# Spectral products of a gated state-space kernel: four real products or three

## The chip, the cores and the metric

The kernel runs on one core of a Trainium2 chip. The metric is the device time of one execution in microseconds. Before the change the median of three executions is 379.08 us (379.05 to 380.93).

## The reference

Two branches read the same input `x` (2048 positions by 1024 channels) and are mixed by a gate. Branch `a` is a diagonal complex state-space recurrence between two projections. Branch `b`, the one the change touches, is a long convolution by FFT:

```python
kv  = k_shift * v                           # k_shift: four taps over k
y_f = rfft(pad(kv)) * rfft(pad(ssm_k))      # complex products, each channel for itself
y   = irfft(y_f)[:S] + kv * ssm_D
b   = x * y
g   = sigmoid((x * gate_w).sum(-1))
out = g * a + (1 - g) * b
```

## The kernel before

**Engines.** TensorE (PE) does the transforms of the convolution as matmuls with tables of cosines and sines, and the projections of branch `a`. VectorE (DVE) does the products of spectra, then the scans of the recurrence. ScalarE (ACT) moves results out of PSUM. SyncE (SP) issues loads and stores, GpSimd (POOL) issues transfers that add into their target (`gather`). Nearly every instruction goes through a helper (`mm`, `tt`, `act`, `move`, `gather`) which chains it behind the one before on its engine, so the order on each engine is the order of the Python text. All these have line 95 in the profile, and are told apart by the tiles they write and read.

**Chunks.** The convolution runs over 8 chunks of 128 channels. The sequence is cut into 4 blocks of 512, and each block is transformed on its own. So a chunk has a spectrum `KH[c]` of the kernel and `VH[c]` of the product k by v, each with a real and an imaginary part, 4 blocks and 512 frequencies: 2 x 4 x 512 elements in each partition. `products(c)` is a complex product and a convolution over blocks at once: output block b sums K block a times V block b - a. The K spectrum already holds the overlap of neighbouring blocks: for chunks 1 to 6 `fwd_K` adds it on PE, for chunk 7 `overlap_K` adds it on DVE (six operations).

**The loop over c = 0 to 6** (line 1190), in which chunk c is multiplied while chunk n = c + 1 is transformed and chunk nn = c + 2 is prepared. `products` and others are generators; `step` runs one up to its next `yield`. In the order of the text, for c from 1:

- `inverse(c - 1)`: 16 matmuls `psz` on the finished spectrum `whole[c - 1]`, which `products(c - 1)` has written over the V spectrum (`Vh` in the profile). The first eight need its first half.
- `step(tv)`: mirror of chunk n's product, `mirror` on PE and `lo` on ACT.
- four steps of `products(c)`, then the rest of `tv`: `ev` on DVE and a gather `ks<-lo`.
- `fwd_K(n)`: matmuls `psk`; the fifth step of `products(c)`; folds of K for nn; the load of `v` for nn, for c = 2 to 4 held by a write of ACT into the tile (`hold`) until ACT gets there; the taps of nn on PE and their copy `ks<-taps` on ACT; loads of k for the chunk after.
- the sixth step, `run(prod)` (the rest), `overlap_K` where it is due, and only then `times_v(nn)`, whose first operation is `ks<-ks,v`: taps of nn times `v` of nn, 2048 elements.
- `fwd_V(n)`: 16 matmuls `psv`, half on `ev`, half on `ks` after its gather; ACT copies them into `Vh`.

Between these stand matmuls of branch `a` (`even`, `odd`). Chunk 7 is multiplied after the loop. There `by_dma` is false and all sums are made on DVE; for chunks 1 to 6 one sum, of 3072 elements `acc<-wkh`, is made by a gather.

**Tiles.** `sums` (`acc` in the profile) has 8192 elements in each partition, `WK` (`wkh`) 7168; `t` is a spare tile. K lies in `BT[2]` or `BT[3]`.

Of the kernel before, what the change touches and what calls it, by code (L numbers as in the profile page):

```python
# [9 lines left out]
ALU = mybir.AluOpType  # L10
ACT = mybir.ActivationFunctionType
BF16 = mybir.dt.bfloat16
# [8 lines left out]
def kernel(  # L21
# [62 lines left out]
    def u4(shape, dt, name):  # L84
        return s5p["wu"].tile(shape, dt, name=name, tag="u4")
# [12 lines left out]
    def mm(o, l, r, first, last):  # L98
        put("pe", nc.tensor.matmul, o, lhsT=l, rhs=r, start=first, stop=last)

    def bc(ap, shape):
        return ap.to_broadcast(shape)
# [3 lines left out]
    def tt(o, a, b, op):  # L106
        put("dve", V.tensor_tensor, out=o, in0=a, in1=b, op=op)
# [19 lines left out]
    def gather(o, i):  # L127
        put("pool", nc.gpsimd.dma_start, out=o, in_=i, accum_op=ALU.add)
# [355 lines left out]
        act(TC[:, 2 * g:2 * g + 2], y, func=ACT.Sin, bias=pih, scale=-TWO_PI)  # L484

    KH, VH = {}, {}

    eos, kss = {}, {}

# [146 lines left out]
    def fwd_K(c, fis=range(NFI)):  # L636
        eo = eos["k", c]
        if c not in KH:
            KH[c] = spectrum("K", c)
        for fi in fis:  # L640
            fsl = slice(fi * 128, (fi + 1) * 128)
            ps = ps2([128, 2, 4, 128], "psk")
            for cc in range(2):
                tab = CF if cc == 0 else SF
                for mt in range(2):
                    mm(ps[:, cc], tab[:, mt, fsl], eo[:, cc, mt], mt == 0, c == NC - 1 and mt == 1)
                for mt in range(0 if c == NC - 1 else 2):
                    tb2 = (SF, NCF)[cc][:, mt, fsl]
                    mm(ps[:, cc, 1:4], tb2, eo[:, 1 - cc, mt, 0:3], False, mt == 1)
            act(of_tile(KH[c], fi), ps, func=ACT.Copy)  # L650
# [15 lines left out]

    def overlap_K(c):

        K = KH[c][0]
        for b in (3, 2, 1):  # L670
            tt(K[:, 0, b], K[:, 0, b], K[:, 1, b - 1], ALU.add)
            tt(K[:, 1, b], K[:, 1, b], K[:, 0, b - 1], ALU.subtract)

    def fwd_V(c, fis=range(NFI)):
        eo = eos["v", c]
# [8 lines left out]
                    mm(ps[:, cc], tab[:, mt, fsl], eo[cc][:, mt], mt == 0, mt == 1)  # L684
            act(of_tile(VH[c], fi), ps, func=ACT.Copy, scale=2.0 / 1024.0)

    def products(c, h=0, home=u4, by_dma=True):

        K, Vt = (x[c][h].rearrange("p c b f d -> p c b (f d)") for x in (KH, VH))
        w = K.shape[3]  # L690
        A = sums[:, :, h * 2048:h * 2048 + 8 * w].rearrange("p k (c b x) -> p k c b x", c=2, x=w)

        def mult(a, t):

            if len(t.shape) == 2:
                t = t.rearrange("p (k y) -> p k y", k=2)
            t = t.rearrange("p k (c b x) -> p k c b x", c=2, x=w)
            k_ = bc(K[:, :, a:a + 1], [128, 2, 8 - 2 * a, w])
            v_ = bc(Vt[:, :, 0:4 - a].rearrange("p c b x -> p c (b x)")[:, None], [128, 2, 2, (4 - a) * w])
            tt(t, k_, v_, ALU.mult)  # L700
            return t

        n1 = WK[:, h * 3072:h * 3072 + 12 * w].rearrange("p (k c b x) -> p k c b x", k=2, c=2, b=3)

        def first(k):

            for f in range(2 if c == 0 and h == 0 else 1):
                x = slice(f * 128, f * 128 + 128) if c == 0 and h == 0 else slice(0, w)
                tt(A[:, k, :, :, x], bc(K[:, k:k + 1, 0:1, x], [128, 2, 4, x.stop - x.start]), Vt[:, :, :, x], ALU.mult)

        def second(k):
            tt(n1[:, k], bc(K[:, k:k + 1, 1:2], [128, 2, 3, w]), Vt[:, :, 0:3], ALU.mult)

        if by_dma:
            first(0)
            yield
            second(0)
            gather(A[:, 0, :, 1:], n1[:, 0])
            yield
            first(1)  # L720
            yield
            second(1)
            if c > 0:
                yield
            tt(A[:, 1, :, 1:], A[:, 1, :, 1:], n1[:, 1], ALU.add)
        else:
            mult(0, sums)
            yield
            mult(1, WK[:, 0:6144])
            yield  # L730
            tt(A[:, :, :, 1:], A[:, :, :, 1:], n1, ALU.add)
        if c > 0:
            yield
        if c > 0:
            n3 = mult(3, home([128, 4 * w], BF16, "t"))
            n2 = WK[:, 3072:7168].rearrange("p (k c b x) -> p k c b x", k=2, c=2, b=2)
            for k in (1, 0):
                tt(n2[:, k], bc(K[:, k:k + 1, 2:3], [128, 2, 2, w]), Vt[:, :, 0:2], ALU.mult)
            yield
            for k in (1, 0):  # L740
                tt(n2[:, k, :, 1:], n2[:, k, :, 1:], n3[:, k], ALU.add)
            tt(A[:, 1, :, 2:], A[:, 1, :, 2:], n2[:, 1], ALU.add)
            yield
            for i in (0, 1):
                tt(A[:, 0, i, 2:], A[:, 0, i, 2:], n2[:, 0, i], ALU.add)
            yield
        else:
            n2 = mult(2, home([128, 8 * w], BF16, "t"))
            n3 = mult(3, home([128, 4 * w], BF16, "t"))
            yield  # L750
            tt(n2[:, :, :, 1:], n2[:, :, :, 1:], n3, ALU.add)
            tt(A[:, 1, :, 2:], A[:, 1, :, 2:], n2[:, 1], ALU.add)
            yield
            tt(A[:, 0, :, 2:], A[:, 0, :, 2:], n2[:, 0], ALU.add)
            yield
        tt(A[:, 1, 1], A[:, 0, 0], A[:, 1, 1], ALU.subtract)
        tt(A[:, 1, 0], A[:, 0, 1], A[:, 1, 0], ALU.add)
        if c == 0 and h == 0:
            return
        t2 = sums[:, 1]  # L760
        if c > 0:
            lo, hi = (A[:, 1, :, :, i * 256:(i + 1) * 256] for i in range(2))
        else:
            lo, hi = (t2[:, i * 2048:(i + 1) * 2048].rearrange("p (c b x) -> p c b x", c=2, x=256) for i in range(2))
        to = whole[c].rearrange("p (a c b x) -> p a c b x", a=2, c=2, b=4)
        tt(to[:, 0], lo, hi, ALU.subtract)
        tt(to[:, 1], lo, hi, ALU.add)

    def inverse(c):

        G = whole.pop(c).rearrange("p (a c b f d) -> p a c b f d", a=2, c=2, b=4, d=128)
        for par in range(2):
            ps = ps2([128, 2, 4, 128], "psz")
            for j in range(2):
                tl = 2 * par + j
                for fi in range(2):
                    for cc, tab in enumerate((CI, SI)):
                        mm(ps[:, j], tab[:, fi, tl * 128:(tl + 1) * 128], G[:, par, 1 - cc, :, fi],
                           fi == 0 and cc == 0, fi == 1 and cc == 1)
            cv = cv_pool.tile([128, 2, 4, 128], BF16, name="cv")  # L780
            act(cv, ps, func=ACT.Copy)
            move(cv_scr[c, :, 2 * par:2 * par + 2], cv)
            yield
# [337 lines left out]
    def step(gen):  # L1121
        next(gen, None)

    def run(gen):
        for _ in gen:
            pass

    def steps(gen, n):
        for _ in range(n):
            step(gen)  # L1130
# [34 lines left out]
    step(turns)  # L1165
    taps(1, dg1)
    step(columns)
    p0 = products(0, 0)
    steps(p0, 3)
    run(columns)  # L1170
    step(sp)
# [18 lines left out]
    for c in range(NC - 1):  # L1190
        n, nn = c + 1, c + 2
        if c == 0:
            load("kn", 2)
            load("kT", 2)
            load("v", 2)
            load_BT(0, 0)
            load_xT(0, (0,))
            p1 = products(0, 1)
            fwd_K(n, (0, 1))
            steps(p0, 2)  # L1200
            run(tv)
            dg = dgs(nn, True)
            steps(p1, 2)
            step(p0)
            step(p1)
            run(p0)
            taps(nn, dg)
            step(sp)
            fwd_K(n, (2, 3))
            step(p1)  # L1210
            step(sp)
            fwd_V(n)
            run(p1)
            run(fold_K(nn))
            tv = times_v(nn)
            step(tv)
            load("kn", 3)
            load("kT", 3)
            load_BT(0, 1)
            apart = spread(3)  # L1220
            step(apart)
            load_xT(0, (1,))
            run(apart)
            continue
# [66 lines left out]
                run(apart)  # L1291
        step(prod)
        run(fk)
        run(prod)
        if n == NC - 1:
            overlap_K(n)
        if nn < NC:
            tv = times_v(nn)
            step(tv)
            step(parts)  # L1300
        else:
            run(next(tiles))
            CT[0] = ld.tile([128, 2, D], BF16, name="CTa", tag="ld")
            hold(CT[0][:, 0, 0:1])
            load_CT(0)
            load_BT(2, 0)
            load_BT(2, 1)
            run(next(tiles))
            run(next(tiles))
# [55 lines left out]

    s5p["last"] = room

    prod, back = products(c, 0, room, False), inverse(c - 1)
    run(old)
    steps(prod, 3)  # L1370
    run(turns_U[3])
    run(next(tiles))
    steps(turning[0], 2)
# [238 lines left out]
```

## Time and profile before

| what | us |
|---|---|
| median of 3 executions | 379.08 |
| the profiled execution, its own time | 381.19 |
| its span, first to last instruction | 379.4 |
| PE busy | 373.6 |
| DVE busy | 368.0 |
| ACT busy | 303.6 |
| POOL busy | 78.0 |

The profile is of one execution, whose own time is 1.8 us above its span, and 2.1 us above the median. In its timeline each row has a start, a length, the engine, the operation with its tiles (out<-in) and shape, how many were merged, and in brackets the idle time ahead of it with what ended it. Lengths of neighbours on an engine overlap by some 0.08 us on DVE and by more on PE, so what an operation costs is the distance from its start to the next one's. The groups give a sum, a mean length and the idle time before. "SPq" rows are issues of transfers; when a transfer has landed stands in the view of DMA issues.

### The profile page before, as it was taken

The page shows a single profiled execution, that of the slowest core. Times are in us where ns is not written, and L with a number is a line of the kernel's source. Part 1 is how long each engine was busy: PE and PEld are TensorE (multiplying, and loading weights), DVE is VectorE, ACT ScalarE, POOL GpSimd, SP SyncE. Part 2 cuts the span into 40 slices and gives each one's busy share as a digit, 9 for nine tenths or more (in the row PEclk, how much of TensorE's full clock was granted, in tenths as well). Part 3 has the DMA queues.
Part 4 walks back from the last instruction along what each step waited for, and adds up shares of the span by engine and source line. Part 5 has one row for each costly group of instructions (what it writes and reads, how often), then busy time and mean ns, then how long its engine had stood idle before and what let it go on. Part 6 is the DMA issues. An engine that isn't in the chain of part 4 may idle for free.

```text
span 379.4 us, 6680 instructions
## 1 busy us (share of the span) xinstructions
PE 373.6 (98%) x2469; PEld 202.4 (53%) x2469; DVE 368.0 (97%) x596; ACT 303.6 (80%) x465; POOL 78.0 (21%) x106
## 2 busy tenths in 40 slices
PE   8999999999999999999999999999999999999996
PEld 5666457566584756754454444444445444444444
DVE  8899999999999999999999999999999999999984
ACT  5779998998989999777999699977979968936301
POOL 4011020020301102022012014122426322532000
PEclk9999999999999999999999999999999999999999
DMA  7879999999999998999999999946999998997223
GB/s 168 162 117 232 209 210 209 226 214 212 223 191 193 214 192 177 187 208 151 188 209 226 228 199 246 211 70 119 185 248 157 268 248 178 189 244 125 57 83 111
DMA packets 125827, 70.99 MB, mean 187 GB/s; under 512 B 104601, under 2 KB 107553, under 8 KB 125794
## 3 DMA queue, kind: packets, MB, share of 16 engines
q1 hardware_dynamic: 112416, 45.90, 55.4%
q0 software_dynamic: 12256, 24.38, 37.8%
q10 hardware_dynamic: 1122, 0.28, 0.4%
q8 instruction: 19, 0.31, 0.3%
q14 instruction: 14, 0.11, 0.1%
HBM read 15.48 MB, written 8.39 MB: 63 GB/s over the span
## 4 chain that ended last, share of the span: by engine, by line
PE 91%; DMA 6%; ACT 2%; SPq 0%; issue 0%; DVE 0%; ACTq 0%
PE psy L95 29%; PE both L95 22%; PE psk L95 10%; PE taps L95 6%; PE psv L95 6%; PE psz L95 5%; PE even L95 4%; PE odd L95 3%; DMA kT<-in_B_k_dram 3%; PE foldk L95 3%; DMA kT<-kT 2%; DMA kB<-kT 1%; ACT Vh L95 1%; PE p L95 1%; PE mirror L95 1%; ACT hr L95 1%
## 5 line engine op out<-in xcount | busy, mean ns | idle before, releaser
L95 PE MATMUL psy<-CT,U 128*128 128x512 bf16 (+1 forms) x426 | 93.2, 374 | 0.0
L95 PEld LDWEIGHTS <-U 128*128 128x128 bf16 x492 | 48.1, 98 | 55.6 <-issue 0.3
L95 PEld LDWEIGHTS <-BT 128*128 128x128 bf16 x544 | 50.5, 98 | 33.5 <-issue 0.2
L95 DVE TENSOR_TENSOR wkh<-BT,Vh 128x2048 bf16<-128x2048 bf16 (+3 forms) x31 | 44.7, 1460 | 0.0
L95 POOL DMA_DIRECT2D U<-Q x26 | 27.1, 1053 | 82.8 <-ACT Q L95 24.8
L95 DVE TENSOR_TENSOR acc<-BT,Vh 128x4096 bf16<-128x4096 bf16 (+3 forms) x19 | 37.0, 1950 | 0.6 <-ACT Vh L95 0.6
L95 ACT ACTIVATE Q<-U,lam 128x512 bf16<-128x512 bf16 (+1 forms) x60 | 35.0, 626 | 2.6 <-issue 1.9
L95 PE MATMUL both<-xT,BT 128*128 128x512 bf16 x160 | 35.3, 379 | 0.0
L95 ACT ACTIVATE Vh<-psv 128x1024 bf16<-128x1024 f32 x32 | 30.7, 1032 | 5.6 <-PE psv L95 5.6
L95 DVE TENSOR_TENSOR_SCAN A<-rv,init,A 128x256 bf16<-128x256 f32 x48 | 34.4, 736 | 0.0
L95 DVE TENSOR_TENSOR acc<-acc,wkh 128x1024 bf16<-128x1024 bf16 (+4 forms) x30 | 32.7, 1130 | 0.1
L95 ACT ACTIVATE BT<-psk 128x1024 bf16<-128x1024 f32 x31 | 30.1, 1037 | 2.3 <-PE psk L95 2.2
L95 ACT ACTIVATE U<-both 128x512 bf16<-128x512 f32 x44 | 24.3, 594 | 8.1 <-PE both L95 7.8
L95 POOL DMA_DIRECT2D acc<-wkh x8 | 9.8, 1219 | 100.2 <-DVE wkh L95 100.2
L95 PE MATMUL psk<-eok,SF 128*128 128x384 bf16 (+1 forms) x120 | 28.5, 354 | 0.0
L95 PEld LDWEIGHTS <-SF 128*128 128x128 bf16 x184 | 18.0, 98 | 18.8
L95 ACT ACTIVATE BT<-psy,gcols 128x1024 bf16<-128x1024 f32 (+1 forms) x6 | 6.3, 1043 | 24.7 <-issue 14.0
L95 PE MATMUL taps<-dg,kT 128*128 128x128 bf16 (+1 forms) x352 | 23.3, 219 | 1.0 <-DMA kT<-kT 0.5
L95 PE MATMUL psz<-Vh,CI 128*128 128x512 bf16 x64 | 24.3, 379 | 0.0
L95 PE MATMUL psz<-Vh,SI 128*128 128x512 bf16 x64 | 24.3, 379 | 0.0
L95 PEld LDWEIGHTS <-kT 128*128 128x128 bf16 x352 | 22.8, 104 | 2.7 <-DMA kT<-in_B_k_dram 1.4
L95 DVE TENSOR_TENSOR U<-U,trn 128x512 bf16<-128x512 bf16 (+1 forms) x60 | 22.0, 391 | 0.1
(225 smaller groups left out, 784.0 us busy)
## 6 DMA issues: line engine op xcount, KB each, us to landing
U<-Q POOLq DMA_DIRECT2D x26, 256.0 KB, 5.2
acc<-wkh POOLq DMA_DIRECT2D x6, 768.0 KB, 8.3
cv_scr<-cv SPq DMA_DIRECT2D x16, 256.0 KB, 3.7
kn<-in_B_ssm_k_dram SPq DMA_DIRECT2D x5, 512.0 KB, 4.4
v<-in_B_v_dram SPq DMA_DIRECT2D x5, 512.0 KB, 5.0
out_dram<-m SPq DMA_DIRECT2D x8, 256.0 KB, 4.6
BT<-cv_scr SPq DMA_DIRECT2D x7, 256.0 KB, 7.2
out_dram<-BT SPq DMA_DIRECT2D x7, 256.0 KB, 2.0
```

What stands on the lines that cost most here:

```text
L95: i = f(*a, **kw)
```

## The change

A complex product of K = (k0, k1) and V = (v0, v1) took four real products. Now, with S = k0 + k1, it takes three: `third` = S·v0, and `both` = k0·(v1 - v0) and k1·(v1 + v0). The imaginary part is third + both[0], the real part third - both[1]. `products_0` keeps the old form for chunk 0. For chunks 1 to 7:

- two sums of V's parts into `Vp` (in `WK`) at the head, one sum of K's parts `S`;
- `both` and `n1`, `n2`, `n3` are pair products of K with `Vp`; `third`, `m1`, `m2`, `m3` are products of `S` with v0; `m1` and `n2` are kept in V's second half, which is free by then;
- the gather for chunks 1 to 6 adds `n1` into `both`; it comes after the third step's product instead of the second's;
- the steps are cut anew. In the loop the sixth is now followed by `times_v(nn)` and its first step, and the last two of `products(c)` come behind it;
- `overlap_K` for chunk 7 makes two operations of 1536 elements into `WK` in place of six of 512 in K; `products(7)` reads them from there.

```diff
-    def products(c, h=0, home=u4, by_dma=True):
+    def products(c, home=u4, by_dma=True):
...
+        tt(Vp[:, 1], Vt[:, 1], Vt[:, 0], ALU.add)
+        tt(Vp[:, 0], Vt[:, 1], Vt[:, 0], ALU.subtract)
+        yield
+        pair(both, 0, 4)
+        yield
+        pair(n1, 1, 3)
+        if by_dma:
+            gather(both[:, :, 1:], n1)
+        if c in K_later:
+            tt(S[:, 0], K[:, 0, 0], K[:, 1, 0], ALU.add)
+            tt(S[:, 1:], later[:, 0], later[:, 1], ALU.add)
         else:
+            tt(S, K[:, 0], K[:, 1], ALU.add)
+        yield
+        t = home([128, 4 * w], BF16, "t")
+        n3, m2, m3 = blocks(t[:, 0:1024], 1, 2), blocks(t[:, 1024:], 2), S[:, 0:1]
+        pair(n3, 3, 1)
+        one(third, 0, 4)
+        yield
+        one(m1, 1, 3)
+        one(m2, 2, 2)
+        if not by_dma:
+            tt(both[:, :, 1:], both[:, :, 1:], n1, ALU.add)
+        one(m3, 3, 1)
+        tt(third[:, 1:], third[:, 1:], m1, ALU.add)
+        yield
+        pair(n2, 2, 2)
+        tt(m2[:, 1:], m2[:, 1:], m3, ALU.add)
+        tt(n2[:, :, 1:], n2[:, :, 1:], n3, ALU.add)
+        tt(third[:, 2:], third[:, 2:], m2, ALU.add)
+        yield
+        tt(both[:, :, 2:], both[:, :, 2:], n2, ALU.add)
+        yield
+        tt(both[:, 1], third, both[:, 1], ALU.subtract)
+        tt(both[:, 0], third, both[:, 0], ALU.add)
+        lo, hi = (both[:, :, :, i * 256:(i + 1) * 256] for i in range(2))
         to = whole[c].rearrange("p (a c b x) -> p a c b x", a=2, c=2, b=4)
         tt(to[:, 0], lo, hi, ALU.subtract)
         tt(to[:, 1], lo, hi, ALU.add)
...
         step(prod)
         run(fk)
-        run(prod)
-        if n == NC - 1:
-            overlap_K(n)
         if nn < NC:
             tv = times_v(nn)
             step(tv)
+        step(prod)
+        if n in apart_K:
+            overlap_K(n)
+        run(prod)
+        if nn < NC:
             step(parts)
         else:
             run(next(tiles))
...
-    prod, back = products(c, 0, room, False), inverse(c - 1)
+    prod, back = products(c, room, False), inverse(c - 1)
     run(old)
-    steps(prod, 3)
+    steps(prod, 4)
```

More of the change, by code (lines that the diff above doesn't have):

```diff
@@ L486 @@
     KH, VH = {}, {}
+    apart_K = (NC - 1,)
+    K_later = {}
     eos, kss = {}, {}
@@ L645, in fwd_K @@
                 for mt in range(2):
-                    mm(ps[:, cc], tab[:, mt, fsl], eo[:, cc, mt], mt == 0, c == NC - 1 and mt == 1)
-                for mt in range(0 if c == NC - 1 else 2):
+                    mm(ps[:, cc], tab[:, mt, fsl], eo[:, cc, mt], mt == 0, c in apart_K and mt == 1)
+                for mt in range(0 if c in apart_K else 2):
                     tb2 = (SF, NCF)[cc][:, mt, fsl]
@@ L667, in overlap_K @@
     def overlap_K(c):
[L669 to L672, printed above, removed]
+        K = KH[c][0].rearrange("p c b f d -> p c b (f d)")
+        t = K_later[c] = WK[:, 4096:7168].rearrange("p (c b x) -> p c b x", c=2, b=3)
+        tt(t[:, 0], K[:, 0, 1:], K[:, 1, 0:3], ALU.add)
+        tt(t[:, 1], K[:, 1, 1:], K[:, 0, 0:3], ALU.subtract)
     def fwd_V(c, fis=range(NFI)):
@@ L685, in fwd_V, with products_0 @@
             act(of_tile(VH[c], fi), ps, func=ACT.Copy, scale=2.0 / 1024.0)
-    def products(c, h=0, home=u4, by_dma=True):
+    def products_0(h):
+        c = 0
         K, Vt = (x[c][h].rearrange("p c b f d -> p c b (f d)") for x in (KH, VH))
@@ L705, in first @@
         def first(k):
-            for f in range(2 if c == 0 and h == 0 else 1):
-                x = slice(f * 128, f * 128 + 128) if c == 0 and h == 0 else slice(0, w)
+            for f in range(2 if h == 0 else 1):
+                x = slice(f * 128, f * 128 + 128) if h == 0 else slice(0, w)
                 tt(A[:, k, :, :, x], bc(K[:, k:k + 1, 0:1, x], [128, 2, 4, x.stop - x.start]), Vt[:, :, :, x], ALU.mult)
@@ L712, in second @@
             tt(n1[:, k], bc(K[:, k:k + 1, 1:2], [128, 2, 3, w]), Vt[:, :, 0:3], ALU.mult)
[L714 to L755, printed above, removed]
+        first(0)
@@ new lines, in products_0 @@
+        yield
+        second(0)
+        gather(A[:, 0, :, 1:], n1[:, 0])
+        yield
+        first(1)
+        yield
+        second(1)
+        tt(A[:, 1, :, 1:], A[:, 1, :, 1:], n1[:, 1], ALU.add)
+        n2 = mult(2, u4([128, 8 * w], BF16, "t"))
+        n3 = mult(3, u4([128, 4 * w], BF16, "t"))
+        yield
+        tt(n2[:, :, :, 1:], n2[:, :, :, 1:], n3, ALU.add)
+        tt(A[:, 1, :, 2:], A[:, 1, :, 2:], n2[:, 1], ALU.add)
+        yield
+        tt(A[:, 0, :, 2:], A[:, 0, :, 2:], n2[:, 0], ALU.add)
@@ L756, in products @@
+        yield
         tt(A[:, 1, 1], A[:, 0, 0], A[:, 1, 1], ALU.subtract)
         tt(A[:, 1, 0], A[:, 0, 1], A[:, 1, 0], ALU.add)
-        if c == 0 and h == 0:
+        if h == 0:
             return
         t2 = sums[:, 1]
-        if c > 0:
-            lo, hi = (A[:, 1, :, :, i * 256:(i + 1) * 256] for i in range(2))
-        else:
-            lo, hi = (t2[:, i * 2048:(i + 1) * 2048].rearrange("p (c b x) -> p c b x", c=2, x=256) for i in range(2))
+        lo, hi = (t2[:, i * 2048:(i + 1) * 2048].rearrange("p (c b x) -> p c b x", c=2, x=256) for i in range(2))
@@ new lines, in products_0, with blocks, Kb, pair @@
+        to = whole[c].rearrange("p (a c b x) -> p a c b x", a=2, c=2, b=4)
+        tt(to[:, 0], lo, hi, ALU.subtract)
+        tt(to[:, 1], lo, hi, ALU.add)
+    def products(c, home=u4, by_dma=True):
+        K, Vt = (x[c][0].rearrange("p c b f d -> p c b (f d)") for x in (KH, VH))
+        w = K.shape[3]
+        area = sums.rearrange("p k y -> p (k y)")
+        def blocks(ap, b, k=None):
+            return ap.rearrange("p (b x) -> p b x", b=b) if k is None else ap.rearrange("p (k b x) -> p k b x", k=k, b=b)
+        both, third, S = blocks(area[:, 0:4096], 4, 2), blocks(area[:, 4096:6144], 4), blocks(area[:, 6144:], 4)
+        Vp = blocks(WK[:, 0:4096], 4, 2)
+        n1 = blocks(WK[:, 4096:], 3, 2)
+        free = Vt[:, 1].rearrange("p b x -> p (b x)")
+        m1, n2 = blocks(free[:, 0:1536], 3), blocks(free, 2, 2)
+        V0 = Vt[:, 0]
+        def Kb(b):
+            return K[:, :, b:b + 1]
+        if c in K_later:
+            n1, later = K[:, :, 1:], K_later[c]
+            def Kb(b):
+                return later[:, :, b - 1:b] if b else K[:, :, 0:1]
+        def pair(o, b, n):
+            tt(o, bc(Kb(b), [128, 2, n, w]), Vp[:, :, 0:n], ALU.mult)
+        def one(o, b, n):
+            tt(o, bc(S[:, b:b + 1], [128, n, w]), V0[:, 0:n], ALU.mult)
+        tt(Vp[:, 1], Vt[:, 1], Vt[:, 0], ALU.add)
+        tt(Vp[:, 0], Vt[:, 1], Vt[:, 0], ALU.subtract)
+        yield
+        pair(both, 0, 4)
+        yield
+        pair(n1, 1, 3)
+        if by_dma:
+            gather(both[:, :, 1:], n1)
+        if c in K_later:
+            tt(S[:, 0], K[:, 0, 0], K[:, 1, 0], ALU.add)
+            tt(S[:, 1:], later[:, 0], later[:, 1], ALU.add)
+        else:
+            tt(S, K[:, 0], K[:, 1], ALU.add)
+        yield
+        t = home([128, 4 * w], BF16, "t")
+        n3, m2, m3 = blocks(t[:, 0:1024], 1, 2), blocks(t[:, 1024:], 2), S[:, 0:1]
+        pair(n3, 3, 1)
+        one(third, 0, 4)
+        yield
+        one(m1, 1, 3)
[4 more added lines that the diff above has]
+        tt(third[:, 1:], third[:, 1:], m1, ALU.add)
+        yield
+        pair(n2, 2, 2)
+        tt(m2[:, 1:], m2[:, 1:], m3, ALU.add)
+        tt(n2[:, :, 1:], n2[:, :, 1:], n3, ALU.add)
+        tt(third[:, 2:], third[:, 2:], m2, ALU.add)
+        yield
+        tt(both[:, :, 2:], both[:, :, 2:], n2, ALU.add)
+        yield
+        tt(both[:, 1], third, both[:, 1], ALU.subtract)
+        tt(both[:, 0], third, both[:, 0], ALU.add)
+        lo, hi = (both[:, :, :, i * 256:(i + 1) * 256] for i in range(2))
@@ L1167 @@
     step(columns)
-    p0 = products(0, 0)
+    p0 = products_0(0)
     steps(p0, 3)
@@ L1197 @@
             load_xT(0, (0,))
-            p1 = products(0, 1)
+            p1 = products_0(1)
             fwd_K(n, (0, 1))
```

## The prediction

> **What bounds the kernel now.** I read the page's busy times first, then what PE waited for, then the order of time on each engine in one pass of the chunk loop.
>
> ```profile
> span 379.4 us, 6680 instructions
> PE 373.6 (98%) x2469; PEld 202.4 (53%) x2469; DVE 368.0 (97%) x596; ACT 303.6 (80%) x465; POOL 78.0 (21%) x106
> ```
>
> PE and DVE are both nearly full, so busy shares do not decide. The view of PE's waits does; this is all of it:
>
> ```profile
> PE raised L95 <- DVE magic L95: 1.2, 1, 1.2
> PE taps L95 <- DMA kT<-in_B_k_dram: 0.5, 1, 0.5
> PE taps L95 <- DMA kT<-kT: 0.5, 1, 0.5
> ```
>
> PE never waits for a product of spectra. Two waits are in the first microseconds, and none belongs to an edited line. The span less PE's busy time is 5.8 us, so that is all that could be won without touching PE's work, and the change leaves PE's instructions and their order alone. DVE can be made faster for nothing; it can be made late at a price.
>
> How late it may be shows in the DVE timeline of one pass, chunk 2:
>
> ```profile
> 70.84 2.29 DVE L95 TENSOR_TENSOR acc<-BT,Vh 128x4096 bf16<-128x4096 bf16 x1
> 73.05 1.75 DVE L95 TENSOR_TENSOR wkh<-BT,Vh 128x3072 bf16<-128x3072 bf16 x1
> ...
> 78.58 0.69 DVE L95 TENSOR_TENSOR ev<-ks,lo 128x1024 bf16<-128x1024 bf16 x1
> 79.19 1.75 DVE L95 TENSOR_TENSOR acc<-acc,wkh 128x3072 bf16<-128x3072 bf16 x1
> 80.86 1.22 DVE L95 TENSOR_TENSOR t<-BT,Vh 128x2048 bf16<-128x2048 bf16 x1
> 81.99 2.36 DVE L95 TENSOR_TENSOR wkh<-BT,Vh 128x2048 bf16<-128x2048 bf16 x2
> 84.26 1.29 DVE L95 TENSOR_TENSOR wkh<-wkh,t 128x1024 bf16<-128x1024 bf16 x2
> 85.47 2.42 DVE L95 TENSOR_TENSOR acc<-acc,wkh 128x2048 bf16<-128x2048 bf16 x3
> 87.81 2.36 DVE L95 TENSOR_TENSOR acc<-acc 128x2048 bf16<-128x2048 bf16 x2
> 90.20 2.36 DVE L95 TENSOR_TENSOR Vh<-acc 128x2048 bf16<-128x2048 bf16 x2
> 92.47 1.22 DVE L95 TENSOR_TENSOR ks<-ks,v 128x2048 bf16<-128x2048 bf16 x1
> 93.67 2.29 DVE L95 TENSOR_TENSOR acc<-BT,Vh 128x4096 bf16<-128x4096 bf16 x1
> ```
>
> The `Vh<-acc` pair is the finished spectrum: its first half is ready at 90.20 + 1.22 = 91.42. PE's inverse of that chunk begins at 92.20, 0.78 us later; here is its first matmul in the four passes that matter, c = 2 to 5:
>
> ```profile
> 92.20 0.38 PE L95 MATMUL psz<-Vh,CI 128*128 128x512 bf16 x1
> 115.55 0.38 PE L95 MATMUL psz<-Vh,CI 128*128 128x512 bf16 x1
> 138.26 0.38 PE L95 MATMUL psz<-Vh,CI 128*128 128x512 bf16 x1
> 161.21 0.38 PE L95 MATMUL psz<-Vh,CI 128*128 128x512 bf16 x1
> ```
>
> **The arithmetic.** Distances between starts give prices: 4096 elements 2.21 (70.84 to 73.05), 3072 1.67, 2048 1.135 (half of 2.27), 1024 0.605, and 0.12 more where an operation reads what the one just before it wrote (87.81 to 90.20 is 2.39, not 2.27). The groups give the two sizes that are missing, less the overlap of 0.08: 1536 costs 0.87, 512 0.335.
>
> ```profile
> L95 DVE TENSOR_TENSOR acc<-acc,wkh 128x1536 bf16<-128x1536 bf16 x2 | 1.9, 958 | 0.1
> L95 DVE TENSOR_TENSOR A<-A,trn 128x512 bf16<-128x512 bf16 x32 | 12.0, 417 | 0.0
> ```
>
> Before, a chunk takes 92.47 - 70.84 = 21.63, of which `ev` is 0.61: 21.02. After, by steps: two sums for `Vp` 2.39; `both` 2.21; `n1` and `S` 2.81; `n3` and `third` 1.74 (9.15 so far); then `ev` 0.61; `m1`, `m2`, `m3` and a sum 2.68 (12.44); `n2` and three sums 2.68 (15.12); the sum into `both` 1.26, the two combinations 2.39, the two halves of the spectrum 2.27. Without `ev` that is 20.43. Three products in place of four save only 0.6 us a chunk, since sums and small operations take their place; chunk 7 with its overlap saves about 1.2. On PE's path that is worth nothing. New operand forms (broadcast `S`, prepared sums) have no row of their own; the nearest, `acc<-BT,Vh` with its broadcast K, is at the same price per element, and I take that.
>
> **What is moved decides.** `ks<-ks,v` of chunk c + 2 now stands ahead of the last six operations of the product. It is 15.12 after the chunk's start, where before it was 21.63. It needs `v`, which has not been loaded by then. SP's issues in the four passes, and two landings, from issue, out of the view of DMA issues (the first and second of them):
>
> ```profile
> 84.29 0.38 SPq L95 DMA_DIRECT2D v<-in_B_v_dram  x1
> 107.09 0.38 SPq L95 DMA_DIRECT2D v<-in_B_v_dram  x1
> 130.79 0.38 SPq L95 DMA_DIRECT2D v<-in_B_v_dram  x1
> 153.93 0.39 SPq L95 DMA_DIRECT2D v<-in_B_v_dram  x1
> ...
> v<-in_B_v_dram SPq DMA_DIRECT2D x1, 512.0 KB, 5.0
> v<-in_B_v_dram SPq DMA_DIRECT2D x1, 512.0 KB, 5.1
> ...
> 134.00:135.00 1.00, 1.00 (x10) 0.82 (x9) 1.00 (x2) 0.38 (x2) 0.00 (x0) 1.00 0.17 28
> ```
>
> The third has no landing shown, but its transfer is over by 134.5, as the DMA engines (share 0.17) have nearly nothing left in that microsecond: 3.7 us. For the fourth I take 4.4, between these. The load cannot come sooner, as ACT lets it go behind the folds of PE:
>
> ```profile
> 84.07 0.20 ACT L95 ACTIVATE v<-pih 128x1 bf16<-128x1 f32 x1
> ```
>
> In chunk 2 DVE arrives at 70.84 + 15.12 = 85.96 and `v` is there at 84.29 + 5.0 = 89.29. DVE stands still for 3.3 us, and queued behind are the sum into `both`, the combinations and the spectrum for which PE waits. From the start of `ks<-ks,v` to the first half of the spectrum is 1.135 + 1.26 + 2.39 + 1.22 = 6.0. So PE's wait at `psz` is landing + 6.0 - start of `psz`:
>
> - chunk 2: 89.29 + 6.0 - 92.20 = 3.09
> - chunk 3: 112.19 + 6.0 - 115.55 = 2.64
> - chunk 4: 134.5 + 6.0 - 138.26 = 2.24
> - chunk 5: 158.33 + 6.0 - 161.21 = 3.12
>
> They add up, 11.1 us, because each `v` is let go by PE's own progress and so shifts with every earlier delay. With 3.7 after the issue for all four it is 7.7, with 5.1 for the last two 13.2. Chunk 1 has its `v` long before. Chunk 6 has no `times_v`.
>
> **The gathers.** The 768 KB gather is issued after 2.39 + 2.21 + 1.67 = 6.27 of DVE work in place of 2.21 + 1.67 = 3.88, 2.39 us later; `ev`, and with it the gather `ks<-lo`, at 9.15 in place of 7.76, 1.39 later. In chunk 1 there is little room:
>
> ```profile
> 55.84 0.91 POOL L95 DMA_DIRECT2D ks<-lo  x1 [3.28 <-DVE ev L95]
> ks<-lo POOLq DMA_DIRECT2D x1, 256.0 KB, 7.1
> ...
> 63.55 0.38 PE L95 MATMUL psv<-ks,SF 128*128 128x512 bf16 x1
> ```
>
> It lands at 62.94, 0.61 ahead of its matmul. Later by 1.39, or by 2.39 if it keeps its place behind the large one, PE waits 0.78 to 1.78 (0 if the queue empties faster); I take 0.8. In chunk 5 the same delay falls within the wait already counted. The large gather also moves 2 us into the time of the `v` loads: 0 to 2 us on each landing, and I take 0.4, nearer to nothing, since after one stalled `psz` DVE and its gathers are early against PE again. Four times: 1.6.
>
> **The clock.** A PE that stands still may lose its clock. The two last windows of the run, and the same 64 matmuls at the start and later, in the chain of waits:
>
> ```profile
> 377.00:378.00 1.00, 0.00 (x0) 0.00 (x0) 0.00 (x0) 0.00 (x0) 0.00 (x0) 1.00 0.22 66
> 378.00:379.40 1.40, 0.00 (x0) 0.00 (x0) 0.00 (x0) 0.00 (x0) 0.00 (x0) 0.56 0.00 0
> ...
> 4.84 5.97 PE taps L95 x64
> 32.87 3.57 PE taps L95 x64
> ...
> 115.71 3.45 PE psz L95 x16
> ```
>
> PE ends at 376; the granted clock (the column ahead of the DMA share) is still 1.00 up to 378 and falls to a mean of 0.56 behind it. So some 2 us without a matmul were enough there, and the stalls are of 2.2 to 3.1. At the start matmuls ran at 5.97 for what takes 3.57 later. If one `psz` group of 3.45 runs at half the clock after a stall, it loses half of 6.9: 3.45; if the clock is back after half the group, 1.73. I take 1.73 after three of the four stalls, 5.2; the bounds are 0 and 4 x 3.45.
>
> [...]
>
> **Sum.** 11.1 + 0.8 + 1.6 + 5.2 = 18.7 us. The profiled execution's 381.19 becomes 399.9; that execution was 2.1 above the median, so the forecast is 379.08 + 18.7 = 397.8.
>
> **Rivals.**
>
> [...]
> - *`v` lands sooner* (0.12): 3.7 after its issue everywhere, as in chunk 4, no clock, no gather: 7.7, 386.8.
> - *The transfers collide* (0.08): the gather holds each `v` back by 2 us, and chunk 1 waits 1.8: 13.2 + 1.8 + 8 = 23, 402.1, and up to 409 with 1.73 of clock four times.
> - *Not slower* (0.05): `v` or DVE is no wait at all, because SP's load gets away ahead of ACT's hold. It decides from a landing at 92.20 - 6.0 = 86.2, 1.9 us after the issue; below that `psz` finds its data, and what is left is PE's own work: 378.6 to 379.1, no change. Nothing shows a load of 512 KB in 1.9.
> - *DVE sets the end* (0.02): then 0.6 x 6 + 1.2 = 4.8 is won, 374.3. For it, 97% busy; against, PE's waits.
>
> **How the numbers follow.** The forecast keeps 0.48. The range of 386.5 to 405 holds it, the two rivals below it and part of the collision; what is left out is the last two and the collision's upper part. Half a percent is 1.9 us, about what a measurement of this kernel tells from no change. Faster by more takes DVE as the bound: 0.02. Within it, the not-slower case: 0.05. Slower: 0.93.
>
> **What would show it.** PE's waits would list `psz` behind DVE's `Vh`, about 3 us each in chunks 2 to 5, and DVE's waits `ks` behind the DMA of `v`, also 2 to 4 us each; chunk 1 would show a wait of `psv` for the gather of `ks`. DVE's busy time would fall by some 5 us while the span grows. The granted clock would be below 1.00 in windows behind the stalls. If `psz` waits for nothing, the step on `v` is wrong; if it does and the clock stays, the third term is; a longer `both<-` row than 2.29 would undo the arithmetic.

## The result and the profile after

| | us |
|---|---|
| before, median of 3 | 379.08 (379.05 to 380.93; a fourth took 385.52) |
| after, median of 4 | 399.76 (396.75 to 400.22) |
| ratio | 1.0512, 95% interval 1.0438 to 1.0586 |
| profiled execution after, its span | 395.0 |

The kernel became 5.1% slower. Executions more than 1.5% above the fastest of their kernel, here the one of 385.52, are left out of every ratio and median. The page after:

```profile
span 395.0 us, 6658 instructions
PE 375.7 (95%) x2434; PEld 201.3 (51%) x2469; DVE 364.1 (92%) x617; ACT 304.4 (77%) x465; POOL 77.5 (20%) x106
```

DVE's work has fallen, 368.0 to 364.1, and the span has grown by 15.6. PE's waits after (us in total, times, longest):

```profile
PE psz L95 <- DVE Vh L95: 10.9, 4, 3.4
PE raised L95 <- DVE magic L95: 1.2, 1, 1.2
PE psv L95 <- DMA ks<-lo: 0.9, 1, 0.9
PE taps L95 <- DMA kT<-in_B_k_dram: 0.8, 1, 0.8
```

The first and third rows are new. DVE's waits give the cause:

```profile
DVE ks L95 <- DMA v<-in_B_v_dram: 13.7, 3, 5.0
DVE ks L95 <- ACT U L95: 3.7, 1, 3.7
```

So `ks<-ks,v` stands still four times. In the second row the view names an ACT row; ACT's copy of the taps had ended before, and the load of `v`, issued at 136.81, was the only other operand. Chunk 2 in the DVE timeline of the changed kernel, and PE's first matmul of that inverse:

```profile
82.77 0.68 DVE L95 TENSOR_TENSOR Vh<-Vh,t 128x1024 bf16<-128x1024 bf16 x1
83.37 0.68 DVE L95 TENSOR_TENSOR acc<-acc,t 128x1024 bf16<-128x1024 bf16 x1
88.23 1.23 DVE L95 TENSOR_TENSOR ks<-ks,v 128x2048 bf16<-128x2048 bf16 x1 [4.18 <-DMA v<-in_B_v_dram]
89.37 1.22 DVE L95 TENSOR_TENSOR acc<-acc,Vh 128x2048 bf16<-128x2048 bf16 x1
90.62 2.36 DVE L95 TENSOR_TENSOR acc<-acc 128x2048 bf16<-128x2048 bf16 x2
93.02 2.36 DVE L95 TENSOR_TENSOR Vh<-acc 128x2048 bf16<-128x2048 bf16 x2
...
94.30 0.61 PE L95 MATMUL psz<-Vh,CI 128*128 128x512 bf16 x1 [3.41 <-DVE Vh L95]
```

DVE is idle for 4.18 with five operations behind it that do not need `v` (the prediction calls them six, but its sum has five). PE begins 94.30 - 88.23 = 6.07 after `ks` does, where the sum from rows of before said 6.0.

The windows of the changed kernel show the second loss (the granted clock is the column before the DMA share):

```profile
91.00:93.00 2.00, 0.00 (x0) 0.00 (x0) 1.99 (x2) 2.00 (x4) 0.00 (x0) 1.00 0.94 308
93.00:100.00 7.00, 5.70 (x14) 2.04 (x15) 6.95 (x6) 3.41 (x7) 0.00 (x0) 0.51 1.03 171
100.00:104.00 4.00, 3.95 (x22) 1.98 (x21) 4.00 (x4) 3.29 (x7) 1.20 (x1) 1.00 0.40 131
...
148.00:151.00 3.00, 3.00 (x8) 1.06 (x7) 3.00 (x3) 0.00 (x0) 0.00 (x0) 0.50 0.59 122
...
175.00:178.50 3.50, 3.30 (x8) 1.16 (x9) 3.50 (x4) 0.00 (x0) 0.19 (x1) 0.51 0.63 141
```

PE is at half clock (0.50 in windows of half a microsecond) behind three of its four waits: for nearly 7 us after the first, 3.4 each after the third and fourth. PE is busy for some 12.2 us of that, in which it does the work of 6.1.

The account: waits 10.9 + 0.9, clock 6.1, together 17.9. The spans differ by less, 15.6, since the profiled execution of before happened to start slower: its first fold began later than that of after, in a part that the change does not touch. Here are the two rows, of before and of after:

```profile
10.85 0.39 PE L95 MATMUL foldk<-ident,kn 128*128 128x256 bf16 x2
```

```profile
9.27 0.61 PE L95 MATMUL foldk<-ident,kn 128*128 128x256 bf16 x4
```

That is 1.6, and 0.5 is the wait of `taps` for `kT<-kT` that before had and after has not: 17.9 - 1.6 - 0.5 = 15.8.

### The profile page after: what moved, and what is told of

It is laid out like the page before. It is cut to its first block, busy times and chain, and to the rows that moved or that the text cites. A ratio compares the mean times of both kernels' runs of the same rounds, so it can differ in the third digit from the quotient of the medians.

```text
span 395.0 us, 6658 instructions
## 1 busy us (share of the span) xinstructions
PE 375.7 (95%) x2434; PEld 201.3 (51%) x2469; DVE 364.1 (92%) x617; ACT 304.4 (77%) x465; POOL 77.5 (20%) x106
## 4 chain that ended last, share of the span: by engine, by line
PE 74%; DVE 13%; DMA 8%; issue 2%; ACT 1%; SPq 0%; DVEq 0%; ACTq 0%
PE psy L95 28%; PE both L95 21%; PE psk L95 8%; PE psz L95 8%; DVE acc L95 7%; DMA v<-in_B_v_dram 5%; PE foldk L95 2%; PE psv L95 2%; PE taps L95 2%; DVE wkh L95 2%; DMA ks<-lo 2%; DVE Vh L95 2%; DVE t L95 1%; DMA kT<-in_B_k_dram 1%; PE even L95 1%
## 5 line engine op out<-in xcount | busy, mean ns | idle before, releaser
L95 PE MATMUL psz<-Vh,CI 128*128 128x512 bf16 x64 | 28.0, 437 | 10.9 <-DVE Vh L95 10.9
L95 ACT ACTIVATE cv<-psz 128x1024 bf16<-128x1024 f32 x16 | 16.0, 1020 | 16.4 <-PE psz L95 16.3
L95 PE MATMUL psz<-Vh,SI 128*128 128x512 bf16 x64 | 27.7, 432 | 0.0
L95 DVE TENSOR_TENSOR acc<-acc,Vh 128x2048 bf16<-128x2048 bf16 (+2 forms) x28 | 26.1, 952 | 0.0
L95 DVE TENSOR_TENSOR ks<-ks,v 128x2048 bf16<-128x2048 bf16 x7 | 8.5, 1215 | 17.4 <-DMA v<-in_B_v_dram 13.7
L95 PE MATMUL taps<-dg,kT 128*128 128x128 bf16 (+1 forms) x352 | 21.2, 207 | 0.9 <-DMA kT<-in_B_k_dram 0.8
L95 PEld LDWEIGHTS <-kT 128*128 128x128 bf16 x352 | 20.6, 98 | 2.5 <-DMA kT<-in_B_k_dram 2.0
```

The source lines that it names most:

```text
L95: i = f(*a, **kw)
```

## The experiments

Each kernel is compared with the kernel before on the same chip; the ratio stands with its 95% interval.

### The new products in the old place

```diff
         step(prod)
         run(fk)
-        if nn < NC:
-            tv = times_v(nn)
-            step(tv)
         step(prod)
         if n in apart_K:
             overlap_K(n)
         run(prod)
         if nn < NC:
+            tv = times_v(nn)
+            step(tv)
             step(parts)
```

> The changed kernel with times_v (the product ks<-ks,v) put back behind run(prod), so with the new products and the old place. Theory (the place of ks ahead of the last six operations makes DVE wait for v): PE's four waits at psz, 10.9 us, and the half clock behind them go; what stays is the later gather in chunk 1, up to 0.9 us: 379.5 to 381.5. Rival (the new products themselves are late, by their operand forms or by the later gather): some of the psz waits stay and the time stays above 385.

Measured: 383.44, ratio 1.0089 (1.006 to 1.0118). The profiled execution is the fastest of twelve, 380.88; PE's two longest waits in it:

```profile
PE psv L95 <- DMA ks<-lo: 2.2, 1, 2.2
PE raised L95 <- DVE magic L95: 1.2, 1, 1.2
```

All waits at `psz` are gone, and the time is below the rival's 385, so the place of one DVE operation made most of the 5.1%. But 0.9% stays, 2 us above what was expected, and a wait for the gather `ks<-lo` of 2.2 stands in the profile, in chunk 5 and not in chunk 1. Five of the twelve executions have a mean granted clock of 0.994 to 0.996; the seventeen of the kernel before have 0.998 to 1.000.

### The old products in the new place

```diff
         run(fk)
-        run(prod)
-        if n == NC - 1:
-            overlap_K(n)
+        step(prod)
         if nn < NC:
             tv = times_v(nn)
             step(tv)
+        run(prod)
+        if n == NC - 1:
+            overlap_K(n)
+        if nn < NC:
             step(parts)
```

> The kernel before, with its four products, and only the place of ks<-ks,v moved: after the seventh step of products(c), with 5.95 us of DVE work from its start to the first half of the spectrum, as in the changed kernel (6.0). Theory: the same waits of PE at psz, about 11 us in chunks 2 to 5, and some 5 to 7 us of half clock, without the wait of psv in chunk 1: 395 to 399. Rival (it is the new products): within 2 us of the kernel before.

Measured: 393.26 (391.52 and 395.0), ratio 1.0357 (1.0315 to 1.0399), at and below the lower end of what was expected. Of PE's and DVE's waits, and the windows behind the stall in chunk 2:

```profile
PE psz L95 <- DVE Vh L95: 9.2, 5, 2.5
...
DVE ks L95 <- DMA v<-in_B_v_dram: 11.4, 4, 3.7
...
93.00:97.00 4.00, 4.00 (x12) 1.45 (x11) 4.00 (x3) 2.96 (x6) 0.00 (x0) 0.57 1.15 198
97.00:100.00 3.00, 3.00 (x17) 1.45 (x16) 3.00 (x3) 2.02 (x3) 1.20 (x1) 1.00 0.62 166
```

Four real products, and the same kinds of waits, with half clock behind. The mean granted clock is 0.987, from which 0.013 x 393.2 / 0.5 = 10.2 us at half clock is an estimate: three stretches of 3.4. So the place alone makes most of the loss, with no new product: 3.6% of the 5.1%. It does not make all of it, as its interval ends below that of the changed kernel (1.0438 to 1.0586). What is missing is near the 0.9% that stayed in the section above, whose cause comes under "The gather": 3.6 and 0.9 are 4.5, within that interval.

### `v` loaded earlier

The load for c = 2 to 4 goes to the head of the pass, with no hold.

```diff
+        if 2 <= c < 5:
+            load("v", nn)
         run(back)
...
-            elif c < 5:
-                load("v", nn, True)
```

> The changed kernel with the loads of v for c = 2 to 4 issued at the head of the pass, some 9 us earlier, with no hold by ACT; chunk 5's load stays. Theory: DVE's waits for v in chunks 2 to 4 go, PE's psz waits there too (2.6 us or so each) with their clock; chunk 5 keeps its 3 us and 1.7 of clock: 399.8 - 8 - 5 = 385 to 388. Rival (the place in the order is too early for DVE whatever v does, or v's transfer only collides elsewhere): three or more psz waits stay, above 393.

Measured: 390.3 (389.46 to 393.88), ratio 1.0303 (1.0261 to 1.0346). This is a miss: better than the changed kernel's 1.0512, but 2 us above the expected range. It is below the rival's 393, though the rival's other sign came: three waits at `psz` stay. Of PE's and DVE's waits in the profiled execution, which took 396.44:

```profile
PE psz L95 <- DVE Vh L95: 7.7, 3, 4.2
...
DVE ks L95 <- ACT ks L95: 5.2, 3, 2.4
DVE ks L95 <- DMA v<-in_B_v_dram: 4.8, 1, 4.8
```

The early loads took away the waits for `v`, all but the last. The expectation had left out the moved operation's other operand: `ks<-ks,v` also needs ACT's copy of the taps, and that comes late as well. The next kernel was made for that; it has the same early loads, and the last `times_v` alone is put behind the product:

```diff
-        if nn < NC:
+        if nn < NC - 1:
             tv = times_v(nn)
             step(tv)
...
         run(prod)
+        if nn == NC - 1:
+            tv = times_v(nn)
+            step(tv)
```

> The changed kernel with the loads of v for c = 2 to 4 at the head of the pass, and only the last times_v (of chunk 7, in pass 5) put back behind run(prod). No ks<-ks,v waits for v any more; in passes 2 and 4 it still waits for its other operand, ACT's copy ks<-taps, which the kernel before ends at 87.79 and 134.29, by which psz would come at 6.0 behind that: 87.79 + 6.0 - 92.20 = 1.6 and 134.29 + 6.0 - 138.26 = 2.0. Theory (both operands of the moved product decide, v first and the taps next): two psz waits, in chunks 2 and 4, of 3.6 us in all, a psv wait of about 1 us in chunk 1 or 5, and 0 to 3.4 of clock: 384 to 388. Rival (v was all): no psz wait, 380 to 382.

Measured: 388.83 beside 382.01 of the kernel before in that session, ratio 1.0143 (1.0046 to 1.0239). Of PE's waits, the first of DVE's, and two windows about the stall in chunk 4:

```profile
PE psz L95 <- DVE Vh L95: 3.5, 2, 2.0
PE psy L95 <- ACT U L95: 2.8, 1, 2.8
...
PE psv L95 <- DMA ks<-lo: 0.5, 1, 0.5
...
DVE ks L95 <- ACT ks L95: 4.7, 3, 2.2
...
138.00:141.00 3.00, 1.13 (x5) 0.51 (x6) 2.97 (x4) 2.76 (x5) 0.00 (x0) 0.98 1.24 219
141.00:144.30 3.30, 3.30 (x9) 1.22 (x8) 3.27 (x3) 1.02 (x1) 0.00 (x0) 0.50 0.67 136
```

Now DVE waits for ACT and no longer for `v`, and PE's two waits are 3.5 in all where 1.6 + 2.0 was worked out. So both operands decide: with `v` there, the taps are next. The time itself cannot be held against the range, as the kernel before was slower in that session; the ratio gives 5.5 us more than before (interval 2 to 9), where the range says 5 to 9. In it is one thing that was not foreseen, in the second row: a wait at `psy`, late in the run, from a gather of branch `a` (`CT<-m`) that landed 14.7 us after its issue here, 7.9 before and 11.8 in the changed kernel. The profiled executions of the two sections above have such late waits too (1.7 at `psy`, 3.1 at `both`); before and the changed kernel have none. Why that gather is late was not tried.

### PE kept at work while it waits

```diff
             ps = ps2([128, 2, 4, 128], "psz")
+            for _ in range(10 if par == 0 and 2 <= c <= 5 else 0):
+                mm(ps[:, 0], CF[:, 0, 0:128], CF[:, 0], True, True)
```

> The changed kernel with ten matmuls of 512 columns added ahead of psz in chunks 2 to 5, whose result is overwritten by the first matmul of psz: 2.16 us of PE work put into the time in which PE would stand still. Theory (the stall costs its own length and the half clock behind it): DVE's waits are as before, PE's wait at psz shrinks to about 1 us, the granted clock stays at 1.00, and the time falls by the 6.8 us that half the 13.7 us at half clock cost: 392 to 394. Rival (the half clock lies within time that PE waits anyhow): 399 to 401; if the filling is work that was not hidden, above 402.

Measured: 393.81 (393.52 to 396.07), ratio 1.0398 (1.0363 to 1.0433). Of PE's waits, and the stretch that was at 0.51 in the changed kernel:

```profile
PE psz L95 <- DVE Vh L95: 5.5, 4, 1.9
...
93.00:100.00 7.00, 6.10 (x30) 2.93 (x30) 6.96 (x6) 5.66 (x11) 0.00 (x0) 1.00 1.06 166
```

Forty matmuls more, and the kernel is faster than the changed one: the half clock was a real loss. The mean granted clock is 1.000 in two of the three executions and 0.995 in the third, where the changed kernel's four have 0.978 to 0.983. It gives back some 4 us by the ratios (1.0512 to 1.0398), not 6.8, as waits and filling are 5.5 + 4 x 2.16 = 14.1 where the waits were 10.9, 3.2 more. The two profiled spans, 395.0 and 392.0, bear that out: 6.1 of clock less 3.2 is 2.9. Chunk 3's wait alone has grown, from 1.48 to 1.95. Three rows of it, the issues of the large gather and of `v` and the end of DVE's wait, with the filling:

```profile
101.54 1.20 POOL L95 DMA_DIRECT2D acc<-wkh  x1 [20.55 <-DVE wkh L95]
107.24 0.38 SPq L95 DMA_DIRECT2D v<-in_B_v_dram  x1
115.10 1.23 DVE L95 TENSOR_TENSOR ks<-ks,v 128x2048 bf16<-128x2048 bf16 x1 [4.90 <-DMA v<-in_B_v_dram]
```

and in the changed kernel:

```profile
101.94 1.20 POOL L95 DMA_DIRECT2D acc<-wkh  x1 [20.75 <-DVE wkh L95]
110.41 0.38 SPq L95 DMA_DIRECT2D v<-in_B_v_dram  x1
115.64 1.22 DVE L95 TENSOR_TENSOR ks<-ks,v 128x2048 bf16<-128x2048 bf16 x1 [5.05 <-DMA v<-in_B_v_dram]
```

With `v` issued 8.5 us behind the gather it is there 5.2 later, with 5.7 us behind it takes 7.9. At full clock PE comes sooner to the point that lets `v` go, and `v` then shares the DMA engines with gathers that are still under way: from 108.5 to 111.5 their queue (q0) took 98% of the engines.

### The gather

What is left of the 0.9% with the old place of `times_v`? In passes 1 and 5 `ev`, and with it the gather `ks<-lo`, was put ahead of the large gather:

```diff
         step(tv)
-        steps(prod, 4)
+        first_steps = 2 if c in (1, 5) else 4
+        steps(prod, first_steps)
         run(tv)
+        steps(prod, 4 - first_steps)
```

> The version with times_v behind (three products, old place), and in passes 1 and 5 the gather ks<-lo issued ahead of the large gather: ev stands after the second step of products(c) instead of the fourth. Theory (what was left over the kernel before, 0.9%, is PE's wait at psv for ks<-lo, which stands in the queue behind the large gather that is now issued 2.4 us later, and the clock that such a wait can cost): no wait of psv, 379 to 381, within 0.5% of before. Rival (the rest comes from the new products or from chunks 2 to 4): it stays at 382 to 385.

Measured: 382.16 beside 380.83 of the kernel before in that session, ratio 0.9994 (0.9945 to 1.0042). All of PE's waits:

```profile
PE raised L95 <- DVE magic L95: 1.2, 1, 1.2
PE psz L95 <- DVE Vh L95: 0.8, 1, 0.8
```

The wait of `psv` is gone, the granted clock is 0.998 or more in all nine executions of the median, and by the ratio the kernel stands level with before. The counterpart delays the large gather in the old kernel:

```diff
             first(0)
             yield
+            if c > 0:
+                first(1)
+                yield
             second(0)
             gather(A[:, 0, :, 1:], n1[:, 0])
             yield
-            first(1)
-            yield
+            if c == 0:
+                first(1)
+                yield
             second(1)
```

> The kernel before with the order first(0), first(1), second(0), gather, second(1) in chunks 1 to 6: the large gather 2.2 us later, all else alike, DVE's work too. Theory (the gather's place alone makes the 0.9%): a wait of psv for ks<-lo of 1 to 2 us in chunk 1 or 5, in some executions with half clock behind it: 380.5 to 384. Rival (it needs the new products): no such wait, within 0.3% of before.

Measured: 384.56, ratio 1.0087 (1.0043 to 1.013), the same 0.9% as with the new products; its times cannot be set beside the expected microseconds, as the kernel before was at 380.83 in that session. The profiled execution, at 398.83 the longest of thirteen, has the expected wait, in chunk 5, beside 10.2 us of late waits on branch `a` (`both` 7.4, `psy` 2.8):

```profile
PE psv L95 <- DMA ks<-lo: 3.5, 1, 3.5
```

Six of the eight executions in the median have a granted clock of 0.994 to 0.996. So the gather's place, with no new product, costs it; how it divides between the wait and the clock was not measured.

### Spending the room on PE's work

With the products no longer late, DVE could take the overlap of chunk 6's K spectrum from PE too (the version with three products and `ks<-lo` first, with `apart_K = (NC - 2, NC - 1)` and `overlap_K` behind `times_v`).

> As the version with ks<-lo first, and the overlap of chunk 6's K spectrum too is added by DVE: 16 matmuls of 384 columns less on PE (2.6 us), two operations of 1536 elements more on DVE (1.7 us). If PE is the bound and DVE's saved 0.6 us a chunk has become room, 377 to 378.5; by my sum the first half of chunk 6's spectrum is ready at 185.1 and psz would come at 184.0, so 1.1 us of the 2.6 go back. Rival (DVE is as full as PE, and every such trade is a wait of psz, with half clock behind): 379 or more.

Measured: ratio 1.0035 (0.9994 to 1.0076), no gain. Of PE's waits:

```profile
PE psv L95 <- DMA ks<-lo: 2.0, 2, 1.2
PE taps L95 <- DMA kT<-kT: 1.6, 1, 1.6
...
PE psz L95 <- DVE Vh L95: 0.5, 1, 0.5
```

In this execution waits for transfers of 3.6 us stand against the 2.6 us of matmuls saved. Neither expectation had that: the wait at `psz` is in chunk 1 and not in chunk 6, and no half clock follows any of them (the mean granted clock is 0.999). The `psv` waits are in passes 3 and 6, where `ks<-lo` still stands behind the large gather. Whether they would go if it were put first there too was not tried. No version tried is faster than the kernel before.

## Why the prediction was right

- *PE sets the pace, DVE's saving is worth nothing.* Right. With the old place and the gather in order the new products give 0.9994, and the interval leaves no room for a gain above 0.6%. DVE's busy time fell by 3.9 us, a little less than the 5 foretold, and nothing came of it.
- *The moved operation waits for `v`, and PE at `psz`.* Right, shown from both sides: by taking the move back, and by making it alone. That the size fits so well is in part luck. The term was 11.1, with 1.6 more for collisions of transfers; 10.9 was measured for both. The four waits were given as 3.09, 2.64, 2.24 and 3.12 and measured as 3.41, 1.48, 3.33 and 2.68, so two are off by more than 1 us, one each way. Chunk 4's came out larger, as its `v` took 4.9 us (136.81 to 141.70) and not 3.7. Chunk 3's came out smaller, as `v` was issued 9.8 us ahead of the moment at which PE was ready for `psz` (110.41, and 121.71 - 1.48 = 120.23), where before it was 8.5 (107.09 to 115.55). In chunk 5 both happened: `v` took 5.3 and not 4.4, and was issued 8.7 ahead and not 7.3. So `v` does not simply shift with PE, as the prediction has it. ACT lets it go, and in chunk 3 ACT was less far behind PE than before: its `hold` came 1.5 us after PE began the last folds (108.73 to 110.19), before 2.6 (104.21 to 106.77).
- *Only `v` decides the place.* Too simple: the prediction did not price the copy of the taps as the next thing to be late. It changed nothing in the forecast, as `v` came last, but it made the expectation for the early load miss.
- *The gather in chunk 1.* 0.8 foretold, 0.9 measured. That in chunk 5 the delay falls within the wait already counted holds for the changed kernel; without that wait it is 2.2 us there.
- *The clock.* 5.2 for three of four stalls was taken, 6.1 was measured, behind three of four; it was mis-sized a little low, since the first stall cost two stretches of half clock (6.8 us). The 1.73 for each was luck: it is half of a `psz` group at half clock, chosen between two bounds without a row that decides, and the stretch turned out to be 3.4 us, which costs 1.7. Of the two signs for it, the end of the run holds (0.56 behind 378.00); the slow taps at the start stay open, as the windows from 0 to 12 of that profile read a granted clock of 1.00 while they ran. Filling the stalls with matmuls kept the clock (1.000 in the profiled execution) and won time (1.0398 for 1.0512). Without this term the prediction's sum is 11.1 + 0.8 + 1.6 = 13.5, or 392.6, a case held at 0.25, the upper one of the two that its range holds below the forecast. Half clock followed waits of 2.7 to 3.4 in the changed kernel, and one of 2.0 in the kernel with early `v` and the last product behind, so the measurement decides against that case.
- *The sum.* 18.7 was forecast, 17.9 is accounted for in the profile. The median of 399.76, for which 397.8 was forecast, stands 20.7 above 379.08. The profiled execution, at 396.75, is the fastest of the four by 2.9; where the other three lose that is not shown.

## What to carry to other kernels

Moving an operation forward on an engine whose order is that of the text moves everything behind it to the arrival of its latest operand (here DVE stood still for 4.18 us with five operations behind that did not need `v`); look up when each operand lands before the move, transfers first, then the copies of other engines. On a pair of full engines a lighter load on the one that does not set the pace bought nothing here (3.9 us less on DVE in the changed kernel, ratio 0.9994 with the gather in order), and the stalls of the other cost more than their length, as its clock fell (10.9 of waits, 6.1 of clock). When a transfer is issued later, look at what stands behind it in the same queue: here PE waited 2.2 at `psv` for the gather `ks<-lo` behind the large one (the new products in the old place).

## What the runs showed of the hardware that was not expected

- In the changed kernel the half clock came in stretches of 3.4 us. The windows 144 to 148, 148 to 151 and 151 to 154 read 0.96, 0.50 and 0.98: 0.3 + 3.0 + 0.1 = 3.4 us at half. In windows of half a microsecond the stretches begin at 93.08, 147.69 and 175.00 and last 6.8, 3.4 and 3.4, so the first is twice as long as the others. The two windows of the kernel with early `v` and the last product behind give 3.4 again (0.1 + 3.3).
- The length of a wait alone did not decide. The wait of 2.0 in chunk 4 of the kernel with early `v` and the last product behind was followed by half clock, from 140.9 on. One of 2.2 (the new products in the old place) was not: the mean granted clock of that execution is 0.999, and 3.4 us at half would have made it 0.996 at most. In the changed kernel the clock fell 2.2, 3.2 and 2.5 us after PE had stopped (at 90.89, 144.45 and 172.52), and after the wait of 1.48 in chunk 3 it did not fall. Here are the windows about that last one:

```profile
120.00:123.00 3.00, 1.52 (x8) 0.60 (x7) 2.97 (x4) 3.00 (x6) 0.00 (x0) 1.00 1.10 173
123.00:127.00 4.00, 3.95 (x20) 1.90 (x20) 3.97 (x3) 4.00 (x7) 0.00 (x0) 1.00 0.91 212
```

What decides, beside the length, was not shown; no run was made to find it.
